# Cached attention, one decode step, twice: V tiles issued from ScalarE's DMA queue, K tiles and weights from SyncE's

## The chip, the cores and the metric

One core of one Trainium2 chip. The metric is the device time of the program in microseconds (us), as a median over several executions.

Some words used throughout. A DMA is a load that an engine issues; a queue is the line in which the loads issued by one engine stand. A packet is one record of the trace's DMA table: a piece of a load, moved by one of the core's 16 DMA engines. A K or V tile, but for the last V, is 128 packets of 32 KiB, 8 for each DMA engine. The completion records tell when each of the 16 DMA engines has finished its share of a load; a tile "lands" with the last of them.

## The reference

Two independent attention blocks, A and B, each decode one token for 8 sequences with a K and a V cache of 4096 positions. Their outputs are concatenated.

```python
# x: (8, 1, 1024)   k_cache, v_cache: (8, 32, 4096, 128)   wq: (1024, 4096)   wo: (4096, 1024)   all bf16
q = (x @ wq).reshape(B, Sq, H, Dh).transpose(0, 2, 1, 3)
scores = einsum("bhqd,bhkd->bhqk", q, k_cache) * Dh ** -0.5
p = softmax(scores)
o = einsum("bhqk,bhkd->bhqd", p, v_cache)
y = o.transpose(0, 2, 1, 3).reshape(B, Sq, H * Dh) @ wo      # out = concat([y_A, y_B], -1)
```

The caches are 4 x 268 MB, and every byte of them is used once. Little arithmetic is done on each, so the kernel is a race to load them.

## The kernel before

The work is cut into 128 steps, n = 0 to 127. A step is one sequence and four heads of one block. It needs one K tile and one V tile, each 128 partitions x 32 KiB (4 MiB). Both kinds share a ring of five slots (160 KiB of every partition), and they go round it in a fixed order, K one step ahead of V:

```python
order = [("k", 0)]
for n in range(NQ):
    if n + 1 < NQ:
        order.append(("k", n + 1))
    order.append(("v", n))
...
def freed(i):                      # what must be done before slot i is written again
    kind, n = order[i]
    return opEacc.get(NR * n + NR - 1) if kind == "k" else opPV.get((n, NR - 1))

def load_tiles():
    while issued[0] < len(order):
        i = issued[0]
        dep = None
        if i >= NSLOT:
            dep = freed(i - NSLOT)
            if dep is None:
                return
        ...
        if i == len(order) - 1:    # the last V comes in four parts
            ...
        else:
            op = dma(to, from_, ("t", i % NSLOT), [dep])
        issued[0] += 1
```

With five slots this means: when K(n-1) has been used, V(n) is issued, and about 1 us later, after the PV product of step n-2, K(n+2).

A step runs as follows. VectorE multiplies K by the broadcast query and folds it (four chunks, some 16 us per tile); TensorE adds up with an identity matrix; VectorE reduces to scores and to their maximum; ScalarE takes the exp; TensorE multiplies by V. In this kernel every engine gets one stream of instructions in program order, and waits in it on semaphores (counters that other engines and finished loads raise).

The weights use the same helper. WQ (2 MiB, in rows of 2 KiB) is loaded for every 16 steps, WO (1 MiB, rows of 2 KiB) for every 8:

```python
def dma(out_ap, in_ap, key, deps):
    return add("sp", lambda e: e.dma_start(out_ap, in_ap), deps, dma_key=key)
...
opWQ[m] = dma(WQ[:], caches[c][3][:, col:col + HM * Dh].rearrange("(k p) n -> p k n", p=128),
              ("wq", 0), [_at(opQ, (m - 1, 1))])
...
opWO[blk] = dma(WO[:], caches[c][4][hb * HQ * Dh:(hb + 1) * HQ * Dh, :].rearrange("(h p) n -> p h n", p=128),
                ("wo", 0), [_at(opProj, blk - 1)])
```

So all loads stand in one line, SyncE's queue.

## Time and profile before

| | |
|---|---|
| time, median of 3 (range) | 2607.15 us (2606.45 to 2608.35) |
| profiled span | 2605.4 us |
| DMA queue, share of 16 engines | 99.4% |
| VectorE busy | 80% |
| read | 1107 MB, 425 GB/s over the span |

The page of the kernel before. The second line gives busy us, share and instructions of each engine. "DMA" and "GB/s" have one figure for each fortieth of the span (9 is 90% or more). The "q1" line has packets, MB and share of 16 engines' span.

```profile
span 2605.4 us, 18877 instructions
...
PE 1384.3 (53%) x7568; PEld 384.2 (15%) x7568; DVE 2085.8 (80%) x1833; ACT 445.6 (17%) x1427; POOL 3.2 (0%) x15
...
DMA  9999999999999999999999999999999999999996
GB/s 409 427 430 431 431 426 430 430 429 431 426 431 430 431 429 428 430 431 429 430 426 429 433 428 432 428 428 431 430 430 422 428 433 428 432 431 431 430 429 295
...
q1 hardware_dynamic: 54160, 1107.38, 99.4%
...
HBM read 1107.33 MB, written 0.03 MB: 425 GB/s over the span
...
```

The one queue is full from start to end. All but the first and last slice lie between 422 and 433 GB/s. No other engine is near that: VectorE, the busiest, has a fifth of its time free.

The waits of the whole run: who waited for whom, us in total, times, longest.

```profile
...
ACT bias L296 <- DVE ngm L290: 1593.4, 127, 19.7
...
DVE ring L261 <- DMA ring<-in_A_k_cache_dram: 247.7, 62, 15.8
...
DVE ring L261 <- DMA ring<-in_B_k_cache_dram: 233.7, 63, 8.7
...
```

VectorE waits for nearly every K tile (125 of 128), 3.9 us on average and never long in the middle: the mark of a loop that the loads pace evenly. ScalarE's wait for the maximum is idle time that costs nothing.

The issue table: destination and source, issuing engine, count, KB each, median us from issue to landing.

```profile
...
ring<-in_B_k_cache_dram SPq DMA_DIRECT2D x64, 4096.0 KB, 40.7
ring<-in_B_v_cache_dram SPq DMA_DIRECT2D x63, 4096.0 KB, 32.1
...
WQ<-in_B_wq_dram SPq DMA_DIRECT2D x4, 2048.0 KB, 44.4
WO<-in_B_wo_dram SPq DMA_DIRECT2D x8, 1024.0 KB, 37.7
```

A tile needs 9.71 us at this rate, as the spacing of the tiles' completion records in the trace shows. A median of 40.7 us from issue to landing therefore says that about three other tiles stood ahead of a K tile in the line. The loads have a reserve.

The end of the chain of waits in order of time: start us, us, what.

```profile
...
2529.92 42.59 DMA ring<-in_B_k_cache_dram
...
2572.53 2.29 DVE ring L261
...
2602.60 0.68 DVE orow L361
```

K127, the last K tile, lands at 2572.5 us and VectorE begins on it at once. From there to the end are 33 us. By the completion records V127 lands at 2592.1 us. VectorE's start on K125 two tiles earlier, for comparison later (start, us, engine, line, operation, and in brackets the idle time before it and what ended it):

```profile
...
2533.67 2.29 DVE L261 TENSOR_TENSOR ring<-ring,qbc 128x4096 bf16<-128x4096 bf16 x1 [5.86 <-DMA ring<-in_B_k_cache_dram]
...
```

Two stretches of 20 us near the end: busy us (and instructions) of each engine, granted TensorE clock, DMA share, GB/s.

```profile
...
core 0: us, PE busy (x) PEld busy (x) DVE busy (x) ACT busy (x) POOL busy (x), PEclk, DMA share, GB/s
...
2540.00:2560.00 20.00, 10.77 (x56) 2.73 (x56) 16.78 (x16) 3.93 (x15) 0.00 (x0) 0.59 1.02 440
...
2580.00:2600.00 20.00, 12.67 (x96) 4.89 (x96) 9.96 (x10) 3.97 (x12) 0.00 (x0) 0.67 0.27 111
...
```

VectorE keeps its usual pace in the first of them. In the second the loads run out.

### The profile page before, as it was taken

What the parts mean: (1) busy time and instruction counts of PE and PEld (TensorE: products, weight loads), DVE (VectorE), ACT (ScalarE), POOL (GpSimd) and SP (SyncE); (2) the same over time, 40 slices, a digit from 0 to 9 for tenths busy, and PEclk for the clock granted to TensorE, in tenths of its full rate; (3) what the DMA queues carried; (4) which work ended last, traced back from release to release, by engine and by line L of the source; (5) the groups of instructions that cost most, each with busy time, mean ns of one, the idle gap of its engine ahead of it and who ended that gap; (6) DMA issues with size and microseconds to landing.
All of it is one profiled execution on the core that took longest, in us unless ns stands there. A gap on an engine that the chain in (4) does not pass through costs nothing.

```text
span 2605.4 us, 18877 instructions
## 1 busy us (share of the span) xinstructions
PE 1384.3 (53%) x7568; PEld 384.2 (15%) x7568; DVE 2085.8 (80%) x1833; ACT 445.6 (17%) x1427; POOL 3.2 (0%) x15
## 2 busy tenths in 40 slices
PE   4455554555545555455554564545545455455545
PEld 1111111111111111111111111111111111111111
DVE  7778887888878878788787887878878787888786
ACT  1112111121112111121111211211112111121111
POOL 0000000000000000000000000000000000000000
PEclk8666665766666666666666666666666666666666
DMA  9999999999999999999999999999999999999996
GB/s 409 427 430 431 431 426 430 430 429 431 426 431 430 431 429 428 430 431 429 430 426 429 433 428 432 428 428 431 430 430 422 428 433 428 432 431 431 430 429 295
DMA packets 54247, 1108.58 MB, mean 425 GB/s; under 512 B 4576, under 2 KB 4608, under 8 KB 21008
## 3 DMA queue, kind: packets, MB, share of 16 engines
q1 hardware_dynamic: 54160, 1107.38, 99.4%
q8 instruction: 59, 0.97, 0.2%
q14 instruction: 28, 0.23, 0.0%
HBM read 1107.33 MB, written 0.03 MB: 425 GB/s over the span
## 4 chain that ended last, share of the span: by engine, by line
DMA 69%; DVE 22%; PE 6%; ACT 1%; issue 1%; SPq 0%
DMA ring<-in_B_k_cache_dram 32%; DMA ring<-in_A_k_cache_dram 30%; DVE ring L261 12%; DVE ring L266 7%; DMA ring<-in_A_v_cache_dram 4%; PE red L274 3%; DVE s_sb L280 3%; DMA ring<-in_B_v_cache_dram 3%; PE pv L316 2%; ACT PM L303 1%; PE o L337 1%; DVE rmax L286 0%; PE proj L356 0%; PE misc L232 0%; ACT accS L322 0%
## 5 line engine op out<-in xcount | busy, mean ns | idle before, releaser
L261 DVE TENSOR_TENSOR ring<-ring,qbc 128x4096 bf16<-128x4096 bf16 x512 | 1165.2, 2276 | 481.4 <-DMA ring<-in_A_k_cache_dram 247.7
L274 PE MATMUL red<-ring,ident 128*128 128x512 bf16 x2048 | 887.1, 583 | 989.4 <-DVE ring L266 989.4
L266 DVE TENSOR_TENSOR ring<-ring 128x2048 bf16<-128x2048 bf16 x512 | 621.1, 1213 | 0.0
L274 PEld LDWEIGHTS red<-ring,ident 128*128 128x128 bf16 x2048 | 213.9, 126 | 1456.3 <-DVE ring L266 1198.7
L316 PE MATMUL pv<-ring,PM 128*16 128x512 bf16 x4096 | 397.7, 504 | 7.2 <-DMA ring<-in_A_v_cache_dram 4.6
L280 DVE TENSOR_REDUCE s_sb<-red 128x32 f32<-128x512 f32 x512 | 349.2, 682 | 16.0 <-PE red L274 16.0
L296 ACT ACTIVATE bias<-ngm 128x1 f32<-128x1 f32 x128 | 26.0, 203 | 1593.5 <-DVE ngm L290 1593.4
L303 ACT ACTIVATE PM<-s_sb,bias 32x128 bf16<-32x128 f32 x512 | 294.9, 576 | 15.2
L330 PE MATMUL o<-E,accS 128*128 128x4 bf16 x512 | 34.0, 171 | 211.1 <-ACT accS L322 211.1
L316 PEld LDWEIGHTS pv<-ring,PM 128*16 128x16 bf16 x4096 | 99.1, 101 | 283.5 <-issue 238.3
L303 ACT ACTIVATION_READ_ACCUMULATOR PM<-s_sb,bias 32x1 f32 x512 | 128.1, 250 | 0.0
L251 ACT ACTIVATE qbc<-misc 128x128 bf16<-128x128 f32 x128 | 35.5, 278 | 385.6 <-PE misc L246 385.6
L322 ACT ACTIVATE accS<-pv 128x512 bf16<-128x512 f32 x128 | 76.5, 597 | 6.3 <-PE pv L316 2.8
L330 PEld LDWEIGHTS o<-E,accS 128*128 128x128 bf16 x512 | 23.4, 106 | 320.1 <-ACT accS L322 320.1
L286 DVE TENSOR_REDUCE rmax<-s_sb 128x1 f32<-128x128 f32 x128 | 36.6, 286 | 4.4
L246 PE MATMUL misc<-q_sb,selb 8*32 8x128 bf16 x512 | 37.3, 282 | 0.8 <-ACT q_sb L237 0.8
L232 PE MATMUL misc<-WQ,xT 128*8 128x512 bf16 x128 | 33.6, 410 | 6.4 <-DMA WQ<-in_A_wq_dram 6.4
L237 ACT ACTIVATE q_sb<-misc 8x512 bf16<-8x512 f32 x16 | 9.4, 587 | 143.8 <-PE misc L232 143.8
L337 PE MATMUL o<-rsum,mask 128*128 128x8 f32 x128 | 29.7, 361 | 0.0
L246 PEld LDWEIGHTS misc<-q_sb,selb 8*32 8x32 bf16 x512 | 13.4, 96 | 106.8 <-issue 106.8
L337 PEld LDWEIGHTS o<-rsum,mask 128*128 128x128 f32 x128 | 28.5, 328 | 0.0
L290 DVE TRANSPOSE_TENSOR_REDUCE ngm<-rmax 128x1 f32<-128x32 f32 x128 | 26.1, 204 | 0.0
(25 smaller groups left out, 59.0 us busy)
## 6 DMA issues: line engine op xcount, KB each, us to landing
ring<-in_A_k_cache_dram SPq DMA_DIRECT2D x64, 4096.0 KB, 39.8
ring<-in_A_v_cache_dram SPq DMA_DIRECT2D x64, 4096.0 KB, 31.5
ring<-in_B_k_cache_dram SPq DMA_DIRECT2D x64, 4096.0 KB, 40.7
ring<-in_B_v_cache_dram SPq DMA_DIRECT2D x63, 4096.0 KB, 32.1
WQ<-in_A_wq_dram SPq DMA_DIRECT2D x4, 2048.0 KB, 40.8
WO<-in_A_wo_dram SPq DMA_DIRECT2D x8, 1024.0 KB, 37.6
WQ<-in_B_wq_dram SPq DMA_DIRECT2D x4, 2048.0 KB, 44.4
WO<-in_B_wo_dram SPq DMA_DIRECT2D x8, 1024.0 KB, 37.7
```

What stands on the lines that cost most here:

```text
L246: i = e.matmul(misc[MP * j:MP * (j + 1), 0:Dh], selb[:, b, :], q_sb[:, blk % 4, j * Dh:(j + 1) * Dh], start=True, stop=True, tile_position ...
L251: "act", lambda e: e.activation(qbc[:, n % 2, :], misc[:, 0:Dh], ACTF.Copy),
L261: opMul[s] = add("dve", lambda e: e.tensor_tensor(v, v, qbc[:, n % 2, :].unsqueeze(1).to_broadcast([128, CT, Dh]), ALU.mult), [opT[("k", n ...
L266: return add("dve", lambda e: e.tensor_tensor(v[:, :, 0:64], v[:, :, 0:64], v[:, :, 64:128], ALU.add), [opMul[s]])
L274: i = e.matmul(dst, ident[:], v[:, :, j, :], start=(j == 0), stop=(j == 3))
L280: opRed[s] = add("dve", lambda e: e.tensor_reduce(s_sb[:, n % 3, r * CT:(r + 1) * CT], red_ps[s % 2][:, :].rearrange("p (t w) -> p t w", w ...
L286: opRmax[n] = add("dve", lambda e: e.tensor_reduce(rmax[:, n % 2:n % 2 + 1], s_sb[:, n % 3, :], AX.X, ALU.max), [opRed[NR * n + NR - 1]])
L303: return e.activation(PM[rows, n % 2, :, j], s_sb[rows, n % 3, :], ACTF.Exp, bias=bias[rows, n % 2:n % 2 + 1], scale=scale, accum_out=rsum ...
L316: i = e.matmul(bank[32 * q:32 * q + 4 * HQ, :], PM[:, n % 2, t:t + 4, :].rearrange("p t j -> p (t j)"), v[:, t * Dh:(t + 4) * Dh], start=( ...
L322: opAcc[n] = add("act", lambda e: e.activation(accS[:, n % 2, :], pv_ps[n % 2][:], ACTF.Copy), [opPV[(n, NR - 1)], _at(opExt, n - 2)])
L330: x = e.matmul(o_ps[blk % 2][:, HQ * b:HQ * (b + 1)], accS[:, n % 2, i * 128:(i + 1) * 128], E16[:, i, :], start=(i == 0), stop=(i == 3))
L337: x = e.matmul(o_ps[blk % 2][:, 64 + B * j:64 + B * (j + 1)], mask[:, j:j + 1].to_broadcast([128, 128]), rsum[:, blk % 2, :], start=True, ...
```

## The change

The intent is to spread the issuing: V tiles go out from ScalarE's queue, while K tiles, weights and the output stay with SyncE. Each stream would then have a line of its own, and neither would wait in the other's. Since a ring slot's semaphore is now raised from two engines, the semaphore counts are given out in the order of the ring.

```diff
--- before.py
+++ after.py
@@ -37,9 +37,13 @@
 
     def __init__(self):
         self.ops = {e: [] for e in ENGINES}
+        self.counts = {}
 
     def add(self, eng, emit, deps=(), dma_key=None):
         op = _Op(eng, emit, list(deps), dma_key)
+        if dma_key is not None:
+            self.counts[dma_key] = self.counts.get(dma_key, 0) + 16
+            op.token = (dma_key, self.counts[dma_key])
         for d in op.deps:
             if not (d.eng == "pe" and eng == "pe"):
                 d.sig = True
@@ -47,13 +51,10 @@
         return op
 
     def tokens(self):
-        counts = {}
+        counts = self.counts
         for e in ENGINES:
             for op in self.ops[e]:
-                if op.dma_key is not None:
-                    counts[op.dma_key] = counts.get(op.dma_key, 0) + 16
-                    op.token = (op.dma_key, counts[op.dma_key])
-                elif op.sig:
+                if op.dma_key is None and op.sig:
                     counts[e] = counts.get(e, 0) + 1
                     op.token = (e, counts[e])
         return counts
@@ -144,8 +145,8 @@
         P = _Program()
         add = P.add
 
-        def dma(out_ap, in_ap, key, deps):
-            return add("sp", lambda e: e.dma_start(out_ap, in_ap), deps, dma_key=key)
+        def dma(out_ap, in_ap, key, deps, eng="sp"):
+            return add(eng, lambda e: e.dma_start(out_ap, in_ap), deps, dma_key=key)
 
 
         def pool_select(view, base, pattern, dep):
@@ -203,9 +204,9 @@
                 if i == len(order) - 1:
                     for r in range(NR):
                         cols = slice(r * CT * Dh, (r + 1) * CT * Dh)
-                        opT[("v", n, r)] = dma(to[:, cols], from_[:, cols], ("vl", r), [dep])
+                        opT[("v", n, r)] = dma(to[:, cols], from_[:, cols], ("vl", r), [dep], "act")
                 else:
-                    op = dma(to, from_, ("t", i % NSLOT), [dep])
+                    op = dma(to, from_, ("t", i % NSLOT), [dep], "act" if kind == "v" else "sp")
                     for r in range(NR):
                         opT[(kind, n, r)] = op
                 issued[0] += 1
```

## The prediction

> **What bounds the kernel.** The loads. The DMA queue table gives the one hardware queue 99.4% of 16 engines' span; the slices show 422 to 433 GB/s from the second to the 39th. 1107 MB are read. The completion records of the K and V tiles, which land in exactly the order of issue, are 9.71 us apart (4 MiB: 432 GB/s), with 15.1 us where a WQ and 12.4 us where a WO lies between. VectorE is second: 80% busy, some 16 us of work per K tile in a period of 19.4 us; the waits table has it 481 us idle on K tiles in 125 waits. ScalarE is 17% busy. The chain of waits is 62% K loads.
>
> **What the change moves.** No byte, no arithmetic. 128 V issues (0.33 us each on SyncE, 42 us in all) go to ScalarE's stream. There each V(n) waits for TensorE's last pass over K(n-1), ahead of the exp of n-1, which needs a VectorE result that comes later than that anyway: in the trace ScalarE waits 13 to 16 us at that place. So the issues hide. Seven V issues of 10 to 16 us, behind a queued WQ, go too; over 20 us of loads are outstanding then, so that brings nothing.
>
> **What should change.** Order, not rate. The Trainium skill, "DMA: Bandwidth & Descriptors", section "Issuing engines are not separate DMA queues", says both queues run on the same 16 engines and only issue time is saved; 0.33 us per 9.71 us tile agrees. A 32 KiB packet takes 1.215 us against 1.214 us of spacing, so I see no idle to fill; I allow at most 0.8% either way for interleaving.
> The same page (section "Queues, rings and completion order") has the engines take turns between queues by packet. So K and V share the rate; weights, now with K alone and in 2 KiB packets, lose against V. Estimates from the durations above: V0 and V1 pass ahead of WQ and K0, so K0 lands at 27 to 36 us instead of 19.4. At each WQ or WO, K comes 5 to 20 us late once, then VectorE runs several tiles without waiting. The outstanding loads at their lowest shrink from some 22 us to 3 to 15 us; I expect no, or only a few us of, idle DMA.
>
> **On the critical path:** the end. Today K127 lands at 2572.5 us, V127 at 2592.1, and the span ends 32.9 us after K127. With shared engines K127 lands 0 to 10 us later, at worst last of all (20 us), with the end of all loads unchanged.  I count +8 us, and +1 for small DMA gaps.
>
> **Prediction: 2616 us**, 8 in 10 between 2600 and 2640. Chances: faster by over 2% 0.02, within 2% 0.91, slower by over 2% 0.07.
>
> **Right if:** the DMA table shows two queues near 49 and 50%, total 98.5 to 99.6%; GB/s of the middle slices within 425 to 434; V's issue-to-landing falls, K's stays near 40 us or grows; VectorE's total wait for K stays near 480 us but in fewer, longer waits (over 10 us); first VectorE work after 25 us; K127 to end still 33 us. **Wrong if** the middle slices fall below 420 (interleaving costs rate) or exceed 434; if DMA shows idle slices (ring starved); if ScalarE's V issues stall for 10 us or more near the weights and delay exp and PV, which TensorE would pass on to VectorE.

## The result, and the profile after

| | before | after |
|---|---|---|
| time, median of 6 (range) | 2607.14 us (2605.49 to 2608.76) | 2622.43 us (2619.95 to 2628.06) |
| profiled span | 2605.4 us | 2618.7 us |
| last V landed (completion records) | 2592.1 us | 2595.5 us |
| K127 landed (completion records) | 2572.5 us | 2575.7 us |
| VectorE began on K127 | 2572.5 us | 2587.5 us |

The ratio is 1.006, with a 95% interval of 1.0047 to 1.0073. A ratio here is the mean time of one kernel's fast runs over that of the other's of the same rounds, so it is not quite the ratio of the medians quoted. The difference is small and real: the ranges do not touch.

The page of the changed kernel. Lines of the source are one further down than before (L261 is now L262).

```profile
span 2618.7 us, 18877 instructions
...
PE 1312.7 (50%) x7568; PEld 368.8 (14%) x7568; DVE 2080.5 (79%) x1833; ACT 445.8 (17%) x1427; POOL 3.2 (0%) x15
...
DMA  9999999999999999999999999999999999999996
GB/s 414 426 432 429 430 431 420 432 429 427 429 427 431 428 425 429 420 431 426 429 431 427 431 430 422 430 426 431 430 422 425 431 430 428 420 432 419 432 430 261
...
q1 hardware_dynamic: 35296, 570.50, 51.1%
q10 hardware_dynamic: 18864, 536.88, 47.9%
...
```

The same bytes now move in two queues, 51.1 and 47.9%. ScalarE has no more work than before. But the line of GB/s has got dents: six slices between the second and the 39th lie at 419 to 422, where before a single one was at 422 and none below.

The waits of the changed kernel:

```profile
...
ACT bias L297 <- DVE ngm L291: 1594.5, 122, 37.8
...
DVE ring L262 <- DMA ring<-in_A_k_cache_dram: 259.4, 33, 30.1
DVE ring L262 <- DMA ring<-in_B_k_cache_dram: 241.5, 27, 26.5
...
```

VectorE's total wait for K has hardly grown (501 us against 481), but it is in 60 waits instead of 125, and the longest are 30 us (at the start) and 28 us. K has become bursty. ScalarE's wait for the maximum is the same to 1 us, so the V issues in its stream did not hold it up; in the trace none of them took longer than 0.49 us.

The issues of block B:

```profile
...
ring<-in_B_k_cache_dram SPq DMA_DIRECT2D x64, 4096.0 KB, 34.6
ring<-in_B_v_cache_dram ACTq DMA_DIRECT2D x63, 4096.0 KB, 26.0
...
WQ<-in_B_wq_dram SPq DMA_DIRECT2D x4, 2048.0 KB, 63.5
WO<-in_B_wo_dram SPq DMA_DIRECT2D x8, 1024.0 KB, 54.9
```

K and V both land sooner than before (34.6 and 26.0 us after issue, against 40.7 and 32.1). The weights pay: WQ goes from 44.4 to 63.5 us, WO from 37.7 to 54.9.

The end of the chain of the changed kernel. (The source of the piece at 2533 was not identified by the view; the next fence names it.)

```profile
...
2533.28 21.76 another core or an unknown queue
...
2555.07 2.29 DVE ring L262
...
2571.31 2.20 DVE ring L262
...
2587.46 2.20 DVE ring L262
...
2615.92 0.68 DVE orow L362
```

VectorE's start on K125 in its timeline, in the same columns as before:

```profile
...
2555.07 2.29 DVE L262 TENSOR_TENSOR ring<-ring,qbc 128x4096 bf16<-128x4096 bf16 x1 [21.79 <-DMA ring<-in_B_k_cache_dram]
...
```

VectorE stands still for 21.8 us because K125 is late. Then it works through K125, K126 and K127 in one go, without another wait for K, as the chain shows: it begins at 2555.07, 2571.31 and 2587.46. K127 had landed at 2575.7 and lay ready for 12 us. Against the kernel before, K125 is begun 21.4 us later and K127 15.0 us later.

The same two stretches as before, in the same columns:

```profile
...
2540.00:2560.00 20.00, 0.53 (x2) 0.26 (x3) 4.90 (x6) 0.40 (x2) 0.00 (x0) 0.50 1.01 436
...
2580.00:2600.00 20.00, 10.92 (x61) 2.92 (x60) 19.97 (x18) 3.39 (x11) 0.00 (x0) 0.67 0.69 290
...
```

VectorE has 4.90 us of work in the first stretch against 16.78 before, while the DMA engines moved 436 GB/s. They had spent the time before on other things than K125. In the second stretch VectorE is full (19.97) and the loads are nearly through.

What these were can be counted in the trace's packet records. The last WO (512 packets of 2 KiB) stands in SyncE's queue between K124 and K125. From 2515.6 to 2532 us, 214 of its packets went out, and 203 packets of V, of 32 KiB each: about one for one, and hardly anything else once K124 was through. When ScalarE's queue ran dry near 2533 us, the other 298 packets of WO went out in some 4 us. Only behind them, from 2534 us on, did packets of K125 follow, and these in turns with V125, which was issued at 2534.4 us; so K125 took until 2555. There the turns can be seen one by one: from 2538 us the packets of V125 and K125 start in nine groups of exactly 16, V, K, V, K and so on, which is one packet of each DMA engine at a time.

So 13.3 us of span split into 3.4 us by which all loads end later, and 9.9 us between the last landing and the end (23.2 us against 13.3).

The theory, A: the engines take turns between the two queues packet by packet, and a weight's packet is 16 times smaller than V's, so V passes and the weight blocks the K tiles behind it in SyncE's queue. In the middle that only reshapes VectorE's waits, apart from some dry moments. At the end it is paid. The rivals: B, two queues cost rate all the time; B', only the dry moments matter; C, issues hold up ScalarE; D, the late start matters. A further one, E, is that K is late because its issues are held up in SyncE's own stream, and the trace of the changed kernel settles it for the end: 20 issues of SyncE took over 1.5 us, up to 23.2 us, but the last of them was over at 2030.5 us, 450 us before the last WO was issued. In the middle, the wait of 22.3 us that ended at 615.9 us came without such an issue too.

The dry moments also stand in the packet records: eight of more than 0.3 us per DMA engine, each beginning 16 to 18 us after a long wait of VectorE has ended. That fits a ring in which no slot comes free while VectorE waits, so that nothing new can be issued; no run tests this reading by itself.

### The profile page after: what moved, and what is told of

Same layout as the page of the kernel before. It is cut to its first block, busy times and chain, and to the rows that moved or that the text cites. A ratio compares the mean times of both kernels' runs of the same rounds, so it can differ in the third digit from the quotient of the medians.

```text
span 2618.7 us, 18877 instructions
## 1 busy us (share of the span) xinstructions
PE 1312.7 (50%) x7568; PEld 368.8 (14%) x7568; DVE 2080.5 (79%) x1833; ACT 445.8 (17%) x1427; POOL 3.2 (0%) x15
## 3 DMA queue, kind: packets, MB, share of 16 engines
q1 hardware_dynamic: 35296, 570.50, 51.1%
q10 hardware_dynamic: 18864, 536.88, 47.9%
## 4 chain that ended last, share of the span: by engine, by line
DVE 48%; DMA 32%; another core or an unknown queue 14%; PE 4%; issue 2%; ACT 1%; SPq 0%
DVE ring L262 27%; DMA ring<-in_A_k_cache_dram 15%; DVE ring L267 14%; DMA ring<-in_B_k_cache_dram 9%; DVE s_sb L281 6%; DMA ring<-in_B_v_cache_dram 5%; DMA ring<-in_A_v_cache_dram 3%; PE red L275 2%; PE pv L317 1%; DVE rmax L287 1%; PE proj L357 0%; ACT PM L304 0%; DVE ngm L291 0%; PE o L338 0%
## 5 line engine op out<-in xcount | busy, mean ns | idle before, releaser
L262 DVE TENSOR_TENSOR ring<-ring,qbc 128x4096 bf16<-128x4096 bf16 x512 | 1165.4, 2276 | 501.0 <-DMA ring<-in_A_k_cache_dram 259.4
L275 PE MATMUL red<-ring,ident 128*128 128x512 bf16 x2048 | 820.9, 545 | 938.8 <-DVE ring L267 938.8
L275 PEld LDWEIGHTS red<-ring,ident 128*128 128x128 bf16 x2048 | 203.7, 121 | 1378.9 <-DVE ring L267 1124.0
L247 PEld LDWEIGHTS misc<-q_sb,selb 8*32 8x32 bf16 x512 | 13.4, 96 | 104.3 <-issue 104.3
## 6 DMA issues: line engine op xcount, KB each, us to landing
ring<-in_B_k_cache_dram SPq DMA_DIRECT2D x64, 4096.0 KB, 34.6
WQ<-in_B_wq_dram SPq DMA_DIRECT2D x4, 2048.0 KB, 63.5
WO<-in_B_wo_dram SPq DMA_DIRECT2D x8, 1024.0 KB, 54.9
```

The source lines that it names most:

```text
L247: i = e.matmul(misc[MP * j:MP * (j + 1), 0:Dh], selb[:, b, :], q_sb[:, blk % 4, j * Dh:(j + 1) * Dh], start=True, stop=True, tile_position ...
L262: opMul[s] = add("dve", lambda e: e.tensor_tensor(v, v, qbc[:, n % 2, :].unsqueeze(1).to_broadcast([128, CT, Dh]), ALU.mult), [opT[("k", n ...
L275: i = e.matmul(dst, ident[:], v[:, :, j, :], start=(j == 0), stop=(j == 3))
```

## The experiments

Every kernel ran in 5 rounds beside the kernel before on the same chip, e1 to e4 on one chip and e5 to e8 on another. The median of before was 2607.36 us for e1 to e4 and 2607.01 us for e5 to e8, against 2607.14 us beside the changed kernel, so that medians can be compared across them within half a microsecond or so. The edits are against the changed kernel. "DMA idle" is counted from the packet records: the time between 3 and 2580 us in which fewer than 16 packets were in flight, summed over the missing ones and divided by 16. It is 1.2 us before and 6.5 us after the change.

### e1: the last eight V tiles back in K's line

```diff
-  opT[("v", n, r)] = dma(to[:, cols], from_[:, cols], ("vl", r), [dep], "act")
+  opT[("v", n, r)] = dma(to[:, cols], from_[:, cols], ("vl", r), [dep], "sp")
...
-  op = dma(to, from_, ("t", i % NSLOT), [dep], "act" if kind == "v" else "sp")
+  op = dma(to, from_, ("t", i % NSLOT), [dep], "act" if kind == "v" and n < 120 else "sp")
```

> The V tiles of the last eight (batch, head-block) steps, n from 120 to 127, go back to SyncE's queue; the other 120 stay on ScalarE's. Theory A (order at the end: the last WO lies ahead of K125 in SyncE's queue, loses its turns to V's packets, K125 lands 22 us late, and VectorE then has three tiles left in a row): K125 lands in time, no wait for K over 12 us in the last 130 us, the span ends about 13 us after the last V landing instead of 23; 2609 to 2613 us, so 9 to 13 us under the changed kernel. Theory B (two queues cost rate or idle the DMA engines all along): stays within 3 us of the changed kernel, 2619 to 2626 us.

Measured: 2611.57 us (2609.73 to 2612.4), ratio 1.0015 to before. VectorE's starts on K125, K126 and K127, with the wait before each:

```profile
...
2537.88 2.29 DVE L262 TENSOR_TENSOR ring<-ring,qbc 128x4096 bf16<-128x4096 bf16 x1 [5.85 <-DMA ring<-in_B_k_cache_dram]
...
2557.30 2.29 DVE L262 TENSOR_TENSOR ring<-ring,qbc 128x4096 bf16<-128x4096 bf16 x1 [3.17 <-DMA ring<-in_B_k_cache_dram]
...
2576.73 2.29 DVE L262 TENSOR_TENSOR ring<-ring,qbc 128x4096 bf16<-128x4096 bf16 x1 [3.19 <-DMA ring<-in_B_k_cache_dram]
...
```

A's figure. Seven eighths of the kernel still run with two queues, and 11 of the 15 us are gone. The span ended 13.4 us after the last V landing (2609.8 and 2596.4). What is left is the later end of all loads: 2596.4 against 2592.1 us. DMA idle is 8.0 us, so the dry moments of the first seven eighths are still there. B' can therefore not be the whole cause: these moments, with the end put right, cost 4.2 us.

### e2: weights on a third queue

```diff
-  ("wq", 0), [_at(opQ, (m - 1, 1))])
+  ("wq", 0), [_at(opQ, (m - 1, 1))], "pool")
...
-  ("wo", 0), [_at(opProj, blk - 1)])
+  ("wo", 0), [_at(opProj, blk - 1)], "pool")
```

> V on ScalarE's queue as in the changed kernel, but WQ and WO issued from GpSimd, a third queue, so no K tile stands behind a weight. Theory A: waits for K over 12 us vanish after the start; K125 in time; 2605 to 2612 us. Theory B, if the rate suffers from taking turns as such: 2615 to 2626 us, as the turns remain. If only starvation at the weights idles the engines (B'), the idle of about 5 us per engine goes too and the last V lands at 2589 to 2593 us instead of 2595.5.

Measured: 2635.65 us (2634.96 to 2637.21, 4 runs), ratio 1.0109. Every time that was expected is missed. The start of its chain of waits shows why (the view does not name the first piece; by the completion records it is the first WQ, which lands at 57.5 us instead of 28.3 in the changed kernel):

```profile
...
7.82 49.71 another core or an unknown queue
57.67 3.59 PE misc L233 x8
62.73 2.30 DVE ring L262
...
```

The first WQ now competes with five tiles on two other queues. TensorE can form the first query at 57.7 us, and VectorE starts at 62.7. By then all five slots are full, and the DMA engines have nothing to do until VectorE has used up K0: from 60 to 80 us the packet records show them idle for the full 20.0 us, and 22.3 us over the run. After 100 us there is no idle window, no wait for K over 12 us, and the busy time of all packets is 2594.6 us per engine against 2593.8 before. So the part after the start speaks against B, but the run as a whole had to be mended: e5.

### e3: weights in V's line, K alone

```diff
-  ("wq", 0), [_at(opQ, (m - 1, 1))])
+  ("wq", 0), [_at(opQ, (m - 1, 1))], "act")
...
-  ("wo", 0), [_at(opProj, blk - 1)])
+  ("wo", 0), [_at(opProj, blk - 1)], "act")
```

> K alone on SyncE's queue; V and both weights on ScalarE's. Theory A: K never stands behind a weight, so no long waits for K; at the end K is in time or early; 2603 to 2612 us, unless V, now behind the weights, comes late to PV. Theory B: 2615 us or more. Rival C (an issue that stalls in ScalarE's stream delays exp and PV): the issue behind a WQ may stall ScalarE for 10 us as it did on SyncE before; then exp and PV wait, and TensorE passes it on to VectorE: 2615 to 2650 us, with waits on V tiles of some 10 us each at the weights.

Measured: 2616.83 us (2612.78 to 2617.13), ratio 1.0032. The waits:

```profile
...
DVE s_sb L281 <- PE red L275: 437.0, 110, 17.3
...
PE pv L317 <- DMA ring<-in_B_v_cache_dram: 244.2, 50, 16.5
...
PE pv L317 <- DMA ring<-in_A_v_cache_dram: 204.3, 50, 17.7
...
DVE ring L262 <- DMA ring<-in_A_k_cache_dram: 20.5, 11, 3.2
...
```

K comes early now: VectorE waits 20.5 us for it in the whole run. V has taken its place as the late one: TensorE waits 448 us for V before PV, and as its stream is in order, VectorE waits 437 us for TensorE's sums. The loss has only moved to the other line. C shows a trace of itself here: by the trace's issue records 13 issues behind a weight took 1.7 to 15.3 us in ScalarE's stream. The changed kernel has none of these in ScalarE's stream, as its weights are on SyncE. This run does not separate how much of its remaining 9.5 us comes from late V and how much from these stalls.

### e4: a control for the start

```diff
-  op = dma(to, from_, ("t", i % NSLOT), [dep], "act" if kind == "v" else "sp")
+  op = dma(to, from_, ("t", i % NSLOT), [dep], "act" if kind == "v" and n >= 2 else "sp")
```

> Only V0 and V1 go back to SyncE's queue. Control for the start: K0 lands at about 19.4 us instead of 38, VectorE starts 19 us earlier. Theories A and B both say that the start does not count, as the loads set the pace: 2618 to 2626 us, within 4 us of the changed kernel. If the late start is what costs (rival D), 2605 to 2612 us.

Measured: 2623.51 us (2621.49 to 2626.44), ratio 1.0061: no gain. VectorE's first work:

```profile
...
19.22 2.29 DVE L262 TENSOR_TENSOR ring<-ring,qbc 128x4096 bf16<-128x4096 bf16 x1 [15.53 <-DMA ring<-in_A_k_cache_dram]
...
```

It starts at 19.2 us instead of 38.0, and the time stays. D is out.

### e5: later weights on the third queue, the first ones as before

The first WQ and WO go from SyncE, all others from GpSimd. Loads from GpSimd have semaphores of their own.

```diff
-  ("wq", 1), ("wo", 1)
+  ("wq", 2), ("wo", 2)          # semaphores
...
-  ("wq", 0), [_at(opQ, (m - 1, 1))])
+  ("wq", 1 if m else 0), [_at(opQ, (m - 1, 1))], "pool" if m else "sp")
...
-  ("wo", 0), [_at(opProj, blk - 1)])
+  ("wo", 1 if blk else 0), [_at(opProj, blk - 1)], "pool" if blk else "sp")
```

> As e2, but the first WQ and the first WO are issued from SyncE as in the changed kernel, so that GpSimd's queue carries only the later weights, which nobody waits for soon. In e2 all 16 DMA engines stood idle from 60 to 80 us, as the first WQ took 87 us on the third queue; that part should go: about 22 us less than e2, 2610 to 2617 us. If taking turns between K and V by itself costs no rate, the last V lands within 2 us of before (2592.1) and DMA idle outside start and end is under 2 us per engine; what then is left over before is the shared end: K127 lands some 10 us ahead of the last V instead of 19.6, +5 to +9 us. If turns cost rate, the last V lands at 2595 us or later.

(The 87 us are the median of block A's four WQ loads in e2. The first landed at 57.5 us, 56 us after its issue.)

Measured: 2611.35 us (2610.2 to 2611.82), ratio 1.0015. The waits of VectorE for K:

```profile
...
DVE ring L262 <- DMA ring<-in_B_k_cache_dram: 228.0, 62, 8.4
...
DVE ring L262 <- DMA ring<-in_A_k_cache_dram: 174.5, 59, 30.0
...
```

The 30.0 us are the start; after it none is over 8.4 us. The last V lands at 2591.8 us and DMA idle is 0.6 us, both a little better than before the change. K and V taking turns, with no weight in K's line, cost no rate: B is out. What is left is the shared end. K127 lands at 2577.1 us, 14.8 us ahead of the last V instead of 19.6, and the median is 4.3 us over before, just under the 5 to 9 expected. Two things changed along with the queue here: a weight's packets from GpSimd are of 4 KiB in the trace, not 2 KiB, and GpSimd issues most WQ loads some 140 us sooner than SyncE did, as no tile stands before them in its stream. The run does not separate these from the queue itself.

### e6: e5 and e1 together

> As e5, with V of n 120 to 127 on SyncE's queue in K's order. If the loss of the changed kernel is weights that lose their turns (idle DMA) plus the order at the end, both are now gone: 2604 to 2609 us, level with before. If anything else of the second queue costs: 2611 us or more.

Measured: 2606.76 us (2604.79 to 2608.28), ratio 0.9996 (0.9983 to 1.0008). The end of its chain of waits:

```profile
...
2531.56 39.92 DMA ring<-in_B_k_cache_dram
...
2601.00 0.68 DVE orow L362
```

The chain ends as that of the kernel before: one load of K up to 2571.5 us and 32 us of work behind it. With both causes gone nothing of the loss is left.

### e7: WO in 8 KiB packets

WO's rows are read in another order, so that each partition gets one run of 8 KiB. The result is wrong; the bytes and the work are the same.

```diff
-  dma(WO[:], caches[c][4][...].rearrange("(h p) n -> p h n", p=128),
+  dma(WO.rearrange("p h n -> p (h n)"), caches[c][4][...].rearrange("(p h) n -> p (h n)", p=128),
```

> The changed kernel with WO read in 8 KiB rows instead of 2 KiB (rows in another order: wrong result on purpose), so 8 packets per engine instead of 32. If the engines take turns between the queues by packet, a WO now gives way to 8 packets of V (10 us) instead of up to 32: the wait for K at a WO falls from about 22 us to 8 to 14 us, at the end too, and the kernel takes 2610 to 2618 us. If they share by bytes, the waits stay (over 18 us) and so does the time, 2619 to 2626 us.

Measured: 2611.41 us (2608.63 to 2612.92), ratio 1.0013. VectorE's start on K125:

```profile
...
2542.83 2.29 DVE L262 TENSOR_TENSOR ring<-ring,qbc 128x4096 bf16<-128x4096 bf16 x1 [15.37 <-DMA ring<-in_B_k_cache_dram]
...
```

The wait for K125 falls from 21.8 to 15.4 us, just outside the 8 to 14 expected, and the time gains 11 us. Same bytes, same queues, a quarter of the packets: that the size of the packets decides is shown, and it fits turns by packet. (After WQ loads, whose packets are still 2 KiB, waits of up to 25.4 us remain.) The run gains in other ways too: DMA idle is 2.2 us, and WO's packets take 40.2 us per DMA engine over the run, against 44.6 us in the changed kernel. The last V lands at 2587.9 us, sooner even than before the change. So part of the 11 us is that all loads end sooner, and some of that has nothing to do with turns; the kernel before was not run with WO in 8 KiB packets.

### e8: one single load moved

Only the last WO goes to GpSimd's queue.

```diff
-  ("wq", 1), ("wo", 1)
+  ("wq", 2), ("wo", 2)          # semaphores
...
-  ("wo", 0), [_at(opProj, blk - 1)])
+  ("wo", blk // (NB - 1)), [_at(opProj, blk - 1)], "pool" if blk == NB - 1 else "sp")
```

> The changed kernel with one single DMA moved: the last WO goes from SyncE's queue to GpSimd's. If this one load ahead of K125 makes the end late, K125 lands before 2545 us, the last wait over 12 us is before 2420 us, and the kernel gains 5 to 10 us: 2612 to 2618 us. If the end is late for another reason: 2619 to 2626 us.

Measured: 2613.89 us (2611.99 to 2615.97), ratio 1.0025. VectorE's starts on K125 and K127:

```profile
...
2540.67 2.29 DVE L262 TENSOR_TENSOR ring<-ring,qbc 128x4096 bf16<-128x4096 bf16 x1 [3.36 <-DMA ring<-in_B_k_cache_dram]
...
2579.55 2.29 DVE L262 TENSOR_TENSOR ring<-ring,qbc 128x4096 bf16<-128x4096 bf16 x1 [3.19 <-DMA ring<-in_B_k_cache_dram]
```

One load of 1 MiB, out of 32 MiB of weights, moved out of K's line returns 8.5 us (2622.43 to 2613.89). The last long wait is gone. The earlier ones are still there, and so is the later end of the loads (2596.7 us).

### The account

The medians lay the loss out in three parts. From before to e5, 4.3 us: K127 shares the engines with the last V tiles. From e5 to e8, 2.5 us: the other weights, in K's line, make K late and the queues dry for a moment (DMA idle 0.6 against 7.6 us). From e8 to the changed kernel, 8.5 us: the last WO makes K125 late where VectorE has no time left to make up. Together that is the whole difference of 15.3 us. The parts add up by construction, as each is the step from one kernel to the next. Each carries an uncertainty of some 2 us, as the ranges of the runs show, and the split depends on the order of the steps: with the end put right first (e1), the dry moments alone cost 4.2 us instead of 2.5. No kernel tried beats the one before: e6 is level with it and needs three queues for that.

## Why the prediction was right or wrong

**The time and the range held**: 2616 predicted, 2622.4 measured, within 2600 to 2640 and within 2%. Some of that is luck: the range is 40 us wide and holds the time before (2607) too, and the sum of +9 us, against +15.3 measured, left out its largest term.

**Loads bound, and the second queue brings no rate: right.** The Trainium skill, "DMA: Bandwidth & Descriptors", section "Issuing engines are not separate DMA queues", says that only issue time is saved; this agrees, with 2591.8 us for the last V in e5 against 2592.1 before. (One slice of the changed kernel, at 419 GB/s, does fall under the 420 that the prediction took as a sign that turns cost rate. By e5 it is not that sign; each of the six slices under 425 GB/s holds one of the eight dry moments.)

**Turns by packet, weights losing against V: right**, and seen directly: 214 packets of WO to 203 of V. K0 landed at 38.0 us; 27 to 36 was the estimate. The long waits for K at the weights were there, 22 to 28 us at all but one of them, somewhat over the 5 to 20 us estimated.

**V issues hide in ScalarE's stream: right**: 0.33 us each, the wait for the maximum unchanged at 1594 us. The long issues behind a weight did not go with the V tiles, though: after the start, 18 issues of K and WO took over 1.5 us on SyncE.

**"I count +8 us" for K127 landing later, and "K127 to end still 33 us": this is the step that failed.** K127 landed only 3.2 us later than before, no more than the loads as a whole (3.4 us). From there to the end took 43.0 us instead of 33. The text had the cause in hand ("K comes 5 to 20 us late once, then VectorE runs several tiles without waiting") but took it for harmless everywhere. The last WO stands in front of the last three K tiles, so K125 was the tile that came late. VectorE, with 16 us per tile, then had three tiles to do in a row, and K127 waited for VectorE and not for a load. The term missing in the sum is the lateness that VectorE had no steps left to work off: 10 us in the profiled run, and 8.5 us in e8, where this one load was moved. The effect that was named, the shared end, is real but measured 4.3 us alone (e5).

**"+1 for small DMA gaps": too small.** DMA idle grew by 5.3 us per engine and the last landing by 3.4 us. With it, the forecast that middle slices stay within 425 to 434 GB/s failed for six of them (419 to 422). That the reserve shrinks at the weights was said; that it runs out after them, eight times, was counted too low.

**K's time from issue to landing: wrong.** It was to stay near 40 us or grow, and fell to 36.0 and 34.6. The weights took up the delay.

## What to carry to other kernels

A second DMA queue adds no bandwidth when the engines are full, but it throws away the order of the loads: small packets in one queue give way to large ones in the other, turn for turn (here 214 of 2 KiB to 203 of 32 KiB), and everything behind them waits. Where loads bound a loop, keep what is needed next in one line, and put large tiles on a second queue only if nothing urgent stands behind small packets in the first; even so, the shared end cost 4.3 us here (e5). Look at the last few steps by themselves: a tile late by some 20 us was nearly absorbed in the middle of this loop, where VectorE has 3 us of slack in each step, and mostly paid at its end (K125 begun 21.4 us later, K127 15.0).

## What the Trainium skill lacked or had wrong

- "DMA: Bandwidth & Descriptors", section "Queues, rings and completion order", says an engine drains a whole packet of typically 9 to 17 descriptors from one queue before switching. Here, with loads from SyncE and ScalarE, the turn was a single row: the 32 KiB rows of V125 and K125 start in nine alternating groups of 16, one row of each DMA engine, and 214 rows of 2 KiB of WO went out against 203 rows of 32 KiB of V (packet records of the changed kernel, from 2538 us and from 2515.6 to 2532 us).
- The same page, "Rules for kernel authors", says that spreading loads over issuing engines doesn't help. It lacks that it can hurt through order: +0.6% here, as the 512 packets of one WO held back a K tile until VectorE had waited 21.8 us for it. With WO in 8 KiB rows (e7) the wait was 15.4 us.
- The same page, section "Why a DMA increments its semaphore by 16 and not by 1", says that a DMA's engines finish independently, but not how far apart. With one queue, the first and last of the 16 completions of a tile drifted from 0.5 us at the start to 11.0 us at the end of the kernel before; with two queues they were 2.3 us apart at K127; that the dry moments let the late ones catch up fits e5, which has none and was 17.0 us apart at K127, but no run tests it by itself.
- The page gives no limit beyond which an issue blocks its engine. Behind a queued weight, issues took up to 15.9 us on SyncE before, up to 23.2 us after, and up to 15.3 us in ScalarE's stream in e3; the median issue took 0.33 us.
